# A fused attention and two expert layers: the first expert's weights loaded at the moment the expert is chosen

## The chip, the core and the metric

The kernel runs on one core of a Trainium2 chip. The core has five engines that run in parallel, each in its own program order: PE (matmul), DVE (vector), ACT (scalar), POOL (GpSimd) and SP (here only an issuer of DMAs). DMAs are issued by SP, by ACT or by POOL and run beside the engines. The metric is device time in microseconds from start to end of one launch, the median of several; less is better.

## The reference

What must be computed, cut to what matters (B=8 batches, H=8 heads, S=576, D=64, 32 packed queries; N=4608 tokens of 512, E=8 experts, F=1024):

```python
p_packed = sm_attn(p, k, v)             # 32 packed queries attend to all keys, per batch and head
x = sm_attn(q, p_packed, p_packed)      # every query attends to the 32 packed results
x = x.transpose(0, 2, 1, 3).reshape(N, 512)

logits = x @ w_gate                     # layer 1: greedy routing over the flattened, sorted logits,
for idx in argsort(-logits.flatten()):  # each token to one expert, at most cap = N // E = 576 per expert
    tok, e = idx // E, idx % E
    if assigned[tok] < 0 and counts[e] < cap: assigned[tok] = e; counts[e] += 1
out[tokens of e] = relu(x @ w1[e]) @ w2[e]

logits = out @ w_gate2 + bias[modality] # layer 2: best expert per token, no capacity
out[tokens of e] = softmax_weight * (relu(x @ w1[e]) @ w2[e])
```

## The kernel before

**Attention.** Function `attention` loops over the eight batches. Each turn of its loop holds several batches at different stages: scores of the packed queries for batch i, the queries' scores for batch i-1, softmax and transposes for batch i-2. The last turn (i = 7) also holds `early()` (line 454), which is `nearest(0, 0, 20)` of the router (lines 670 to 678): seven DVE steps that find, for the first 20 of 36 token columns, the best expert, its code and the four bytes of its logit. It stands ahead of `pack_D` (line 242, tile `dup`) and of the transposition in `sm_aT` (line 338). After the loop the rows of attention's result are made: `out_rows` multiplies on PE (line 367), copies the result to the tile `xm` on ACT (line 370) and stores it to the DRAM tensor `xs` with a DMA on SP's queue (line 372): 40 stores, five for each batch.

**Routing.** `Router.phase(k)` finds the k-th expert to be filled: `nearest`, then `search`, eight rounds of one threshold comparison on DVE (`ge`), a count on PE (line 654), sums on DVE (`two`, `cp`), a second PE product (line 1008, `cp` with `oner`) and a reduction on DVE (`cmx`). After round eight the expert's number is written to `ex`. Then a list of its tokens (`idx`) is made. All these steps are recorded and have line 1008 where they are emitted later.

**Experts.** `forward` runs units: units 0 to 7 are the experts of layer 1 in the order in which they are chosen, later units are blocks of layer 2. For a unit POOL gathers its rows from `xs` into tile `G` (line 1263), PE transposes them (line 1300), ACT and DVE split them in a high and a low part, XH and XL (lines 1301 and 1302). The weights come as raw chunks of 512 KB into four buffers, `raw`; ACT copies a chunk to the high part (w1H, line 1460), and DVE (or POOL for w2) subtracts to get the low part (w1L, line 1466). The products of the first matrix are on line 1517, those of the second on line 1572; results of the first are evacuated by ACT and DVE (lines 1492 and 1494), those of the second by ACT (line 1577). For unit 0 the four chunks of the first matrix are loaded as 16 DMAs of 128 KB (line 1407), issued by SP after it has read the expert's number from `ex` into a register (line 1229).

**What sets the order.** The program is emitted once, by a list scheduler (`Sched`) that keeps a modelled time for each engine: whenever modelled PE time goes on (`advance`), it takes ready steps from its chains (routing, splits, gathers) and puts them between the products. Order on each engine is fixed then; on the chip an engine that comes to a step whose data isn't there waits, with all behind it. `due` is the modelled time at which a chunk has landed, `GLAND` (8.5) the modelled time between the first gather and unit 0's first transposes.

**Memory and semaphores.** `raw` lies in the pool `m_w`, which is opened after attention's pools are closed, so it lies on memory that attention's tiles held; its first DMA waits for all that used them, the row stores of line 372 among it. The completions of DMAs issued by SP and ACT are counted on eight semaphores, DMAHW0 to DMAHW7, that are given out in turn in program order over both queues; a DMA first waits until the one that had its semaphore before it has landed.

Of the kernel before, what the change touches and what calls it, by code (L numbers as in the profile page):

```python
# [7 lines left out]
F32 = mybir.dt.float32  # L8
# [9 lines left out]
B, H, S, D, NP = 8, 8, 576, 64, 32  # L18
N, DM, E, F = 4608, 512, 8, 1024
# [40 lines left out]
def attention(tc, ctx, cn, q, k, v, p, w_gate, xs, LG, middle, early):  # L60
    nc = tc.nc
# [273 lines left out]
    def sm_aT(b):  # L335
        T, mx, T3 = Ts.pop(b)
        a = new_aT(b)
        nc.vector.transpose(out=a, in_=T)
        aT[b] = a
# [21 lines left out]
    def out_rows(b, c, ring, hook=None):  # L361
        ahead(b, c)
        n = 128 if c < 4 else 64
        dst = wk.tile([128, 4, 4, 32], F32, name="xm", bufs=5)[:n]
        t = ring.tile([128, 4, 4, 32], F32, name="tr")[:n]
# [5 lines left out]
        to = xs[b * S:b * S + 512].rearrange("(p m) d -> m p d", m=4)[c] if c < 4 else xs[b * S + 512:(b + 1) * S]  # L371
        nc.sync.dma_start(to, dst.rearrange("p a c i -> p (a c i)"))
        if c == 4:
# [9 lines left out]
    todo = [(b, c) for b in range(B) for c in range(5)]  # L383
# [18 lines left out]
    for i in range(B):  # L402
# [43 lines left out]
        if p1 and SM == 1:  # L446
            sm_max(i - 1)
            sm_sub(i - 1, nc.gpsimd)
        if EARLY and not n1 and EP == 1:
            early()  # L450
        pack_v(i)
        fill(FILL[2])
        pack_D(i)
        if p2 and AT == 0:
            sm_aT(i - 2)
        if AP == 2:
            ahead(*todo[0])
# [673 lines left out]
BYROW = 5  # L1131
EARLY = 20
EP = 1
# [15 lines left out]

def forward(tc, ctx, cn, R, R2, wg2, S, P, todo, rows, closing, xs, ys, lst, out, m1_w1, m1_w2, m2_w1, m2_w2):  # L1150
    nc = tc.nc
# [9 lines left out]
    def more_phases():  # L1161
        k = phase_k[0]
        if k < E and k <= min(started[0] + 3, P.coded + 2):
            phase_k[0] += 1
            P.add(k)

    for b, c in todo:
        half = 0.44 + (SLACK1 if P.coded >= 0 else SLACK) / 2
        rows(b, c, lambda: S.advance(half))
        S.advance(half)  # L1170
# [4 lines left out]
    W = {n: wp.tile([128, 4096], F32R, name="w" + n) for n in ("1H", "1L", "2H", "2L")}  # L1175
    raw = wp.tile([128, 4, 1024], F32, name="raw")
    raws = [raw[:, i] for i in range(4)]
    mp = ctx.enter_context(tc.tile_pool(name="m_ps", bufs=1, space=PSUM))
# [17 lines left out]
    gathered, l1_done, lg_done = [0], [-1], [-1]  # L1196
    free = list(raws)
    queue = []
    landed, due = {}, {}

    class Unit:
# [16 lines left out]
        def prepare(self):  # L1218
# [8 lines left out]
            else:  # L1227
                t, i = R2.tb[:, 0], self.u - E
            self.e = nc.values_load(t[0:1, i:i + 1], engines=[SP], min_val=0, max_val=E - 1)
            if not self.one:  # L1230
# [17 lines left out]
                if self.last:  # L1248
                    cm.ops.append(("vector", 0.1, lambda: nc.vector.tensor_copy(sa, Ma[:, :, 1]), t))
            for which in (1, 2):  # L1250
                queue.extend((self, which, c) for c in range(4))
# [146 lines left out]
    def fetch():  # L1398
        while queue and free:
            u, which, c = queue[0]  # L1400
            w = ((m1_w1, m1_w2) if u.one else (m2_w1, m2_w2))[which - 1]
            if which == 1 and (not u.u or 2 <= u.u < BYROW):
                queue.pop(0)
                t = free.pop(0)
                rows = w[bass.ds(u.e, 1)].rearrange("o (c a i) f -> a c i (o f)", a=4, i=32)[c]
                for i in range(4):
                    nc.sync.dma_start(t[32 * i:32 * i + 32], rows[i])
                landed[u.u, which, c] = t
                due[u.u, which, c] = S.t["sync"] = max(S.t["sync"], S.t["tensor"] + (2 if u.u else LAND)) + 2.2
                continue  # L1410
# [279 lines left out]
def tile_attention_moe(ctx, tc, q, k, v, p, m1_wg, m1_w1, m1_w2, mod_id, m2_wg, m2_bias, m2_w1, m2_w2, out):  # L1690
# [7 lines left out]
    LG = rp.tile([128, NT, E], F32, name="LG")  # L1698
    HL = rp.tile([128, 2, NT], BF16, name="HL")
    wg2 = rp.tile([128, 4, 32], F32, name="wg2")  # L1700
    ctx.enter_context(tc.manual_schedule())
# [19 lines left out]
    P.add(0)  # L1721
    forward(tc, ctx, cn, R, R2, wg2, S, P, todo, rows, attn.close, xs, ys, lst, out, m1_w1, m1_w2, m2_w1, m2_w2)

# [21 lines left out]
```

## Time and profile before

| | us |
|---|---|
| time, median of 3 runs (lowest, highest) | 1134.14 (1133.48, 1136.73) |
| the profiled execution's own time | 1134.52 |
| its span, first to last instruction | 1132.8 |
| PE busy | 1041.8 (92%) |
| DVE busy | 713.5 (63%) |
| POOL busy | 488.7 (43%) |
| ACT busy | 444.6 (39%) |

The profile is of one execution. Attention fills the first 189 us of the span, layer 1 goes from 213 to about 702, layer 2 from there to the end. A share over the whole span says little about a stage; the views below are therefore of stretches. The chain of waits is followed back from the last instruction, at each step to what released it; read forward it tells which work set the end.

### The profile page before, as it was taken

The numbers are of one execution on the slowest core, as the hardware profiler recorded it, in microseconds if no ns is written. First come the engines' busy times: TensorE is split into PE (matmuls) and PEld (weight loads), VectorE is DVE, ScalarE is ACT, GpSimd is POOL, SyncE is SP. The second block draws the span as 40 slices with busy tenths as digits, with TensorE's granted clock in tenths as the row PEclk, the third lists the DMA queues.
The fourth block names the chain that finished last, engine by engine and source line by source line (L and its number), as shares of the span: only waits on it lengthen the run. The fifth ranks groups of instructions, "written<-read, shape, count | busy, mean of one in ns | idle before, by whom it ended". The sixth has DMA issues, their size and how long they took to land.

```text
span 1132.8 us, 24490 instructions
## 1 busy us (share of the span) xinstructions
PE 1041.8 (92%) x9152; PEld 967.9 (85%) x9152; DVE 713.5 (63%) x2105; ACT 444.6 (39%) x940; POOL 488.7 (43%) x595
## 2 busy tenths in 40 slices
PE   6689797699899998999999999989999999999996
PEld 4577664588888897989999999979898999999995
DVE  1468777688979889884556566655555556455430
ACT  4467564323332323333434334333443433434331
POOL 1123301212424224047565344477787778742401
PEclk9899899699999999999999999999999999999998
DMA  9989246633243242224345343554445454433301
GB/s 257 278 228 259 53 168 201 158 75 117 64 139 113 80 137 57 99 89 145 117 134 138 99 145 93 135 143 126 126 144 143 106 170 136 127 125 102 99 20 43
DMA packets 117857, 146.90 MB, mean 130 GB/s; under 512 B 55946, under 2 KB 80522, under 8 KB 116704
## 3 DMA queue, kind: packets, MB, share of 16 engines
q1 hardware_dynamic: 102368, 116.43, 35.9%
q0 software_dynamic: 13776, 28.76, 8.7%
q8 instruction: 74, 1.21, 0.5%
q14 instruction: 55, 0.45, 0.2%
q10 hardware_dynamic: 1584, 0.05, 0.1%
HBM read 116.31 MB, written 29.52 MB: 129 GB/s over the span
## 4 chain that ended last, share of the span: by engine, by line
PE 60%; DVE 12%; issue 9%; DMA 9%; POOL 5%; ACT 2%; SPq 2%; POOLq 0%; ACTq 0%; DVEq 0%
PE mm L1572 26%; PE mm L1517 22%; DMA G<-ys,gi 4%; POOL out_dram L1344 3%; PE sc L170 2%; POOL G L1282 2%; PE tr L367 1%; DMA raw<-in_moe_w_dram 1%; PE sc L367 1%; DVE hL L1494 1%; DMA G<-xs,idx 1%; DMA vm<-in_v_dram 1%; PE tr L150 1%; DVE cmx L1008 1%; PE b L150 1%
## 5 line engine op out<-in xcount | busy, mean ns | idle before, releaser
L1517 PE MATMUL mm<-XH,w1H 128*128 128x290 f32 (+3 forms) x1024 | 306.9, 300 | 8.7 <-ACT XH L1301 3.8
L1517 PE MATMUL mm<-XL,w1H 128*128 128x290 f32 (+3 forms) x1024 | 307.9, 301 | 0.5 <-DVE XL L1321 0.3
L1517 PE MATMUL mm<-XH,w1L 128*128 128x290 f32 (+3 forms) x1024 | 305.4, 298 | 2.8 <-DVE w1L L1466 2.7
L1572 PE MATMUL mm<-hH,w2H 128*128 128x288 f32 (+3 forms) x768 | 231.9, 302 | 1.1 <-ACT YT L1577 1.1
L1572 PE MATMUL mm<-hH,w2L 128*128 128x288 f32 (+3 forms) x768 | 232.7, 303 | 0.0
L1572 PE MATMUL mm<-hL,w2H 128*128 128x288 f32 (+3 forms) x768 | 231.7, 302 | 0.1
L1492 ACT ACTIVATE hH<-mm 128x290 fp32r<-128x290 f32 (+3 forms) x256 | 105.7, 413 | 293.4 <-PE mm L1517 279.6
L1517 PEld LDWEIGHTS mm<-XH,w1H 128*128 128x128 f32 x1024 | 195.2, 191 | 11.2 <-ACT XH L1301 4.2
L1517 PEld LDWEIGHTS mm<-XH,w1L 128*128 128x128 f32 x1024 | 195.4, 191 | 3.9 <-DVE w1L L1466 3.5
L1517 PEld LDWEIGHTS mm<-XL,w1H 128*128 128x128 f32 x1024 | 194.7, 190 | 1.6 <-DVE XL L1321 0.8
L1494 DVE SCALAR_TENSOR_TENSOR hL<-mm,hH 128x290 fp32r<-128x290 f32 (+3 forms) x256 | 115.2, 454 | 116.7 <-ACT hH L1492 115.6
L1282 POOL DMA_INDIRECT G<-ys,gi x152 | 158.2, 1041 | 62.8 <-issue 31.7
L1572 PEld LDWEIGHTS mm<-hH,w2H 128*128 128x128 f32 x768 | 144.5, 188 | 1.6 <-ACT YT L1577 1.5
L1572 PEld LDWEIGHTS mm<-hL,w2H 128*128 128x128 f32 x768 | 144.5, 188 | 0.3 <-DVE hL L1494 0.3
L1572 PEld LDWEIGHTS mm<-hH,w2L 128*128 128x128 f32 x768 | 144.4, 188 | 0.1
L1344 POOL DMA_INDIRECT out_dram<-Y,si x93 | 96.1, 1033 | 112.0 <-DVE Y L1542 48.5
L1466 POOL TENSOR_TENSOR w2L<-raw,w2H 128x512 fp32r<-128x512 f32 x48 | 63.2, 1338 | 172.2 <-ACT w2H L1460 172.1
L1577 ACT ACTIVATE YT<-mm 128x288 f32<-128x288 f32 (+2 forms) x96 | 39.9, 419 | 203.8 <-PE mm L1572 202.1
L1308 DVE STREAM_TRANSPOSE XT<-G 128x128 f32<-128x128 f32 x206 | 55.6, 295 | 83.6 <-DMA G<-ys,gi 62.0
L1466 DVE TENSOR_TENSOR w1L<-raw,w1H 128x512 fp32r<-128x512 f32 x128 | 83.8, 677 | 19.6 <-ACT w1H L1460 19.0
L1460 ACT ACTIVATE w1H<-raw 128x512 fp32r<-128x512 f32 x128 | 73.1, 623 | 19.5 <-DMA raw<-in_moe_w_dram 11.5
L1460 ACT ACTIVATE w2H<-raw 128x512 fp32r<-128x512 f32 x128 | 73.1, 622 | 0.0
(383 smaller groups left out, 1544.3 us busy)
## 6 DMA issues: line engine op xcount, KB each, us to landing
raw<-in_moe_w_dram SPq DMA_DIRECT2D x112, 512.0 KB
ys<-Y SPq DMA_DIRECT2D x8, 1152.0 KB
qm<-in_q_dram SPq DMA_DIRECT2D x8, 1024.0 KB
vm<-in_v_dram SPq DMA_DIRECT2D x8, 1024.0 KB
xs<-xm SPq DMA_DIRECT2D x32, 256.0 KB
raw<-in_moe_w_dram SPq DMA_DIRECT2D x64, 128.0 KB
km<-in_k_dram SPq DMA_DIRECT2D x7, 1024.0 KB
G<-ys,gi POOLq DMA_INDIRECT x152
```

The source lines that it names most:

```text
L150: nc.tensor.transpose(t[:, i, :], src[:, h + i // 2, 128 * (i % 2):128 * (i % 2) + 128], ident)
L170: nc.tensor.matmul(t[32 * c:32 * c + 32, :512].rearrange("p (i j n) -> p j i n", i=2, j=2)[:, j], lhs(h, j), m[:, h], start=True, stop=Tru ...
L1282: nc.gpsimd.indirect_dma_start(out=G[:, g], out_offset=None, in_=ys[:n], in_offset=bass.IndirectOffsetOnAxis(ap=self.gi[:, g:g + 1], axis= ...
L1308: nc.vector.transpose(out=self.x[0][:, :, 32 * g:32 * g + 32], in_=G[:, g].rearrange("p (c i) -> p c i", c=4))
L1344: i = nc.gpsimd.indirect_dma_start(out=to, in_=rows, in_offset=None, out_offset=bass.IndirectOffsetOnAxis(ap=at, axis=0), bounds_check=to. ...
L1460: nc.scalar.activation(a, b, AF.Copy)
L1466: (nc.gpsimd if pool else nc.vector).tensor_tensor(p[0], p[1], p[2], op=OP.subtract)
L1492: nc.scalar.activation(hh, t, AF.Relu)
L1494: ch.ops.append(("vector", 0.37, lambda: nc.vector.scalar_tensor_tensor(hl, t, 0.0, hh.bitcast(F32), op0=OP.max, op1=OP.subtract), ts + 0.2))
L1517: nc.tensor.matmul(t, a[:, c, fs], b[:, c, s], start=(i == 0), stop=(i == 11))
L1572: nc.tensor.matmul(t, l, r, start=(i == 0), stop=(i == 23))
L1577: nc.scalar.activation(YT[:, d, s], t, AF.Copy)
```

## The change

It has three parts. The raw buffers get memory of their own (pool `r_s`, opened at the start). `first_loads` issues the expert's number and the 16 loads of unit 0 when phase 0 has chosen its expert (`P.hooks` are called by `choose`), and the row stores of the last batch go to ACT's queue. `early()` stands after `pack_D` and `sm_aT`.

```diff
-        nc.sync.dma_start(to, dst.rearrange("p a c i -> p (a c i)"))
+        (nc.scalar if b == B - 1 else nc.sync).dma_start(to, dst.rearrange("p a c i -> p (a c i)"))
...
-        if EARLY and not n1 and EP == 1:
-            early()
         pack_v(i)
         fill(FILL[2])
         pack_D(i)
         if p2 and AT == 0:
             sm_aT(i - 2)
+        if EARLY and not n1 and EP == 1:
+            early()
...
+    raws = [raw[:, i] for i in range(4)]
+    queue, landed, due, one_e = [], {}, {}, []
+
+    def load_rows(u, e, c, t):
+        w = m1_w1 if u < E else m2_w1
+        rows = w[bass.ds(e, 1)].rearrange("o (c a i) f -> a c i (o f)", a=4, i=32)[c]
+        for i in range(4):
+            nc.sync.dma_start(t[32 * i:32 * i + 32], rows[i])
+        landed[u, 1, c] = t
+        due[u, 1, c] = S.t["sync"] = max(S.t["sync"], S.t["tensor"] + (2 if u else LAND)) + 2.2
+
+    def first_loads():
+        if one_e or 0 not in P.experts:
+            return
+        one_e.append(nc.values_load(R.ex[0:1, 0:1], engines=[SP], min_val=0, max_val=E - 1))
+        for c in range(4):
+            load_rows(0, one_e[0], c, raws[c])
+
+    P.hooks.append(first_loads)
...
-    raw = wp.tile([128, 4, 1024], F32, name="raw")
-    raws = [raw[:, i] for i in range(4)]
...
-    free = list(raws)
-    queue = []
-    landed, due = {}, {}
+    free = []
...
-            for which in (1, 2):
+            for which in (1, 2) if self.u else (2,):
                 queue.extend((self, which, c) for c in range(4))
...
+    raw = rp.tile([128, 4, 1024], F32, name="raw")
```

On SP, at the end of attention, the last two row stores stand ahead of the expert's number and the first load. Before:

```order
L372 DMA xs_70<-xm_2427 128x512 [waits DMAHW6_49,Activation_49]
L372 DMA xs_70<-xm_2435 64x512 [waits DMAHW7_49,Activation_49]
L1229 TENSOR_LOAD ex_378 [waits DVE_49]
L1229 ISA x2
L1407 ISA
L1407 DMA raw_2458<-in_moe_w1_dram 32x1024 [waits DMAHW3_49,DMAHW2_49,DMAHW4_49,DMAHW1_49,DMAHW5_49,DMAHW0_49,DMAHW6_49,DVE_49,DMAHW7_49,PE_49,Pool_49]
```

The same place on SP in the changed kernel; the two stores are the last of batch 6, and the loads are those of line 1407 before (ISA rows put the register into a DMA's address):

```order
L372 DMA xs_70<-xm_2383 128x512 [waits DMAHW1_49,Activation_49]
L372 DMA xs_70<-xm_2392 64x512 [waits DMAHW2_49,Activation_49]
L1181 TENSOR_LOAD ex_379 [waits DVE_49]
L1181 ISA x2
L1174 ISA
L1174 DMA raw_78<-in_moe_w1_dram 32x1024 [waits DMAHW4_49]
L1174 ISA
L1174 DMA raw_78<-in_moe_w1_dram 32x1024 [waits DMAHW6_49]
```

The five stores of the last batch are gone from SP's order and the first load waits for one semaphore. On ACT they stand each behind its copy of line 370, ahead of the first w1H. In the order of both queues the stores and the loads take the semaphores in turn: of the 16 loads (counted from 0), load 3 waits for the last store of batch 6, loads 5, 7, 9 and 11 for the second to the fifth store of batch 7, the others for earlier loads.

On DVE, in the last turn of attention's loop (`best`, `rw`, `mxc`, `sign`, `key`, `digits` are the nearest-expert step), before:

```order
L319 TENSOR_REDUCE mx<-T 128x36
L670 TENSOR_REDUCE best_1874<-LG 128x20
L671 TENSOR_TENSOR rw<-LG,best_1874 128x160
L672 TENSOR_TENSOR rw<-rw,w8b 128x160
L673 TENSOR_REDUCE mxc_1875<-rw 128x20
L675 TENSOR_SCALAR sign<-best_1874 128x20
L677 TENSOR_TENSOR key<-best_1874,sign 128x20
L678 CAST digits_1876<-key 128x4x20
L242 TENSOR_SCALAR dup<-b_66,st 128x128 x2
L338 STREAM_TRANSPOSE qm<-T 128x1152
```

The same place in the changed kernel:

```order
L319 TENSOR_REDUCE mx<-T 128x36
L242 TENSOR_SCALAR dup<-b_66,st 128x128 x2
L338 STREAM_TRANSPOSE qm<-T 128x1152
L670 TENSOR_REDUCE best_1920<-LG 128x20
L671 TENSOR_TENSOR rw<-LG,best_1920 128x160
L672 TENSOR_TENSOR rw<-rw,w8b 128x160
L673 TENSOR_REDUCE mxc_1921<-rw 128x20
L675 TENSOR_SCALAR sign<-best_1920 128x20
L677 TENSOR_TENSOR key<-best_1920,sign 128x20
L678 CAST digits_1922<-key 128x4x20
```

The seven steps stand behind `dup` and the transposition instead of ahead of them.

On DVE, where unit 0 begins (w1L is the low part of its weights, XL of its rows, hL of its first results; the other rows are rounds of the search for the second expert), before:

```order
L1008 TENSOR_SCALAR w<-w,sel_f 128x36
L1008 TENSOR_TENSOR ge<-w,tab 128x15x5x8
L1466 TENSOR_TENSOR w1L<-raw,w1H 128x512
L1008 TENSOR_TENSOR two<-b_66,own 128x64
L1466 TENSOR_TENSOR w1L<-raw,w1H 128x512 x4
L1302 TENSOR_TENSOR XL<-mm_2462,XH 128x4x128
L1302 TENSOR_TENSOR XL<-mm_2463,XH 128x4x128
L1008 TENSOR_REDUCE two_2113<-two 128x8
L1494 SCALAR_TENSOR_TENSOR hL<-mm_2464,hH 128x256
```

The same place in the changed kernel (lines 1477, 1318 and 1505 are 1466, 1302 and 1494 before):

```order
L1008 TENSOR_TENSOR cp<-two_2114,fold_361 128x120
L1477 TENSOR_TENSOR w1L<-raw,w1H 128x512
L1008 TENSOR_REDUCE cmx<-b_66 128x15
L1008 SCALAR_TENSOR_TENSOR cmx,sel_f<-cmx,onef 128x15
L1477 TENSOR_TENSOR w1L<-raw,w1H 128x512 x4
L1318 TENSOR_TENSOR XL<-mm_2488,XH 128x4x128
L1318 TENSOR_TENSOR XL<-mm_2489,XH 128x4x128
L1008 TENSOR_SCALAR wt<-w,sel_f 128x36
L1505 SCALAR_TENSOR_TENSOR hL<-mm_2490,hH 128x256
```

Before, three rounds and the first part of a fourth stand ahead of unit 0's first XL; in the changed kernel it is one round and most of a second. From the second half of unit 4 on, both orders are the same on every engine.

## Rows read from the trace of the kernel before

**Rows 1.** Chain of waits, end of attention to unit 0: start us, us, what.
```profile
189.34 3.44 DMA xs<-xm
...
192.92 0.38 SPq L1407
...
196.98 6.26 DMA raw<-in_moe_w_dram
203.26 6.70 DMA raw<-in_moe_w_dram
...
210.72 1.29 DVE w1L L1466 x2
212.02 1.21 DVE XL L1302 x2
...
213.27 2.93 PE mm L1517 x12
```

**Rows 2.** Stretches: length, busy us by engine, PEclk, DMA share, GB/s.
```profile
184.30:188.60 4.30, 4.30 (x21) 3.02 (x20) 3.54 (x16) 2.59 (x5) 0.00 (x0) 1.00 0.62 218
188.60:192.90 4.30, 1.08 (x39) 0.97 (x38) 4.01 (x18) 0.59 (x1) 0.00 (x0) 1.00 0.47 154
...
197.30:203.30 6.00, 1.82 (x12) 1.15 (x12) 4.15 (x14) 1.15 (x2) 2.31 (x3) 0.50 0.98 217
203.30:207.70 4.40, 1.66 (x11) 1.53 (x12) 2.54 (x8) 1.15 (x2) 0.00 (x0) 0.50 1.03 241
```

**Rows 3.** Timeline of DVE, the last attention turn: start us, us, instruction [idle before].
```profile
132.31 0.30 DVE L670 TENSOR_REDUCE best<-LG 128x20 f32<-128x160 f32 x1
...
135.85 0.60 DVE L242 TENSOR_SCALAR dup<-b,st 128x128 f32<-128x128 f32 x2
136.37 1.37 DVE L338 STREAM_TRANSPOSE qm<-T 128x1152 f32<-128x1152 f32 x1
```

**Rows 4.** Timelines of ACT and PE, the same turn.
```profile
134.62 1.16 ACT L326 ACTIVATE T<-T 128x1152 f32<-128x1152 f32 x1 [0.62 <-POOL T L323]
137.04 0.78 ACT L256 ACTIVATE qz<-tr 64x256 f32<-64x256 f32 x2 [1.25 <-PE tr L250]
...
138.93 0.62 PE L170 MATMUL sc<-qT,qz 128*32 128x256 f32 x2
```

**Rows 5.** Timelines of DVE and POOL, an earlier attention turn.
```profile
90.95 0.60 DVE L242 TENSOR_SCALAR dup<-tr,st 128x128 f32<-128x128 f32 x2
...
91.11 2.13 POOL L323 TENSOR_TENSOR T<-T,mx 128x1152 f32<-128x1152 f32 x1 [2.34 <-DVE mx L319]
```

**Rows 6.** Timelines of DVE and SP, an expert's number and the loads behind it.
```profile
183.35 0.15 DVE L1008 TENSOR_SCALAR ex<-code 128x1 int32<-128x1 f32 x1
...
241.93 0.14 DVE L1008 TENSOR_SCALAR ex<-code 128x1 int32<-128x1 f32 x1
...
243.03 1.90 SPq L1417 DMA_DIRECT2D raw<-in_moe_w_dram  x4
```

**Rows 7.** Timeline of ACT: a DMA issue, last row copy, unit 1's weights.
```profile
131.21 0.41 ACTq L1008 DMA_DIRECT2D wg<-in_moe_w_gate_dram  x1
...
188.72 0.59 ACT L370 ACTIVATE xm<-sc 64x512 f32<-64x512 f32 x1 [0.41 <-PE sc L367]
...
257.99 1.14 ACT L1460 ACTIVATE w1H<-raw 128x512 fp32r<-128x512 f32 x2
```

**Rows 8.** Timeline of POOL: the first gather; of DVE: two rounds' comparisons.
```profile
193.69 1.36 POOL L1263 DMA_INDIRECT G<-xs,idx  x1 [49.09 <-DVE oh L1008]
...
193.56 0.46 DVE L1008 TENSOR_TENSOR ge<-w,tab 128x600 bf16<-128x600 bf16 x1
196.77 0.47 DVE L1008 TENSOR_TENSOR ge<-w,tab 128x600 bf16<-128x600 bf16 x1
```

**Rows 9.** Stretches: unit 0's and unit 3's first halves, columns as in rows 2.
```profile
213.00:248.00 35.00, 32.27 (x243) 31.18 (x243) 26.04 (x84) 11.28 (x26) 10.23 (x8) 0.94 0.17 41
...
417.00:452.00 35.00, 29.40 (x282) 27.87 (x273) 33.35 (x124) 9.78 (x23) 16.10 (x18) 1.00 0.27 78
```

More of the change, by code (lines that the diff above doesn't have):

```diff
@@ L1147, with forward @@
 LCAP = N + -(-IG // 2) * 64
-def forward(tc, ctx, cn, R, R2, wg2, S, P, todo, rows, closing, xs, ys, lst, out, m1_w1, m1_w2, m2_w1, m2_w2):
+def forward(tc, ctx, cn, R, R2, wg2, S, P, raw, todo, rows, closing, xs, ys, lst, out, m1_w1, m1_w2, m2_w1, m2_w2):
     nc = tc.nc
@@ L1228, in prepare @@
                 t, i = R2.tb[:, 0], self.u - E
-            self.e = nc.values_load(t[0:1, i:i + 1], engines=[SP], min_val=0, max_val=E - 1)
+            self.e = (nc.values_load(t[0:1, i:i + 1], engines=[SP], min_val=0, max_val=E - 1) if self.u
+                      else one_e[0])
             if not self.one:
@@ L1401, in fetch @@
             w = ((m1_w1, m1_w2) if u.one else (m2_w1, m2_w2))[which - 1]
-            if which == 1 and (not u.u or 2 <= u.u < BYROW):
+            if which == 1 and 2 <= u.u < BYROW:
                 queue.pop(0)
[L1404 to L1409, printed above, removed]
+                load_rows(u.u, u.e, c, free.pop(0))
                 continue
@@ L1721, in tile_attention_moe @@
     P.add(0)
-    forward(tc, ctx, cn, R, R2, wg2, S, P, todo, rows, attn.close, xs, ys, lst, out, m1_w1, m1_w2, m2_w1, m2_w2)
+    forward(tc, ctx, cn, R, R2, wg2, S, P, raw, todo, rows, attn.close, xs, ys, lst, out, m1_w1, m1_w2, m2_w1, m2_w2)
 _INS = ["q", "k", "v", "p", "moe_w_gate", "moe_w1", "moe_w2", "moe2_modality_id", "moe2_w_gate", "moe2_modality_bias",
```

## The prediction

> **What bounds the kernel now.** I read the chain of waits first, around the end of attention, and then the table of stretches and the timelines of single engines for the price of each link. The chain runs through a gap [rows 1]: the last row store is issued at 189.34 and lands 3.44 us later, SP issues the first weight load at 192.92, two spans of weight loads follow (6.26 and 6.70 us, to 209.96), then the last w1L and XL, and PE begins unit 0 in earnest at 213.27. From 197.3 to 207.7 PE is busy for 3.5 of 10.4 us, at a granted clock of 0.50, the 1.2 GHz level, while the DMA engines are busy all the time at 217 to 241 GB/s [rows 2]. So a load of 2.1 MB holds everything. It could start earlier: the expert's number is written at 183.50 [rows 6], 9.4 us before the first load, which only waits because its buffer lies on attention's memory. While attention ends, the DMA engines are 0.62 busy [rows 2]; there is room.
>
> **The moved step.** All times here and below are on the clock of the trace before. The nearest-expert step occupies DVE from 132.31 until `dup` starts at 135.85, 3.54 us [rows 3]. Then come the transposes of `dup`, ACT's two `qz` copies at 137.04 and PE's next scores at 138.93 [rows 4]. Without the step ahead of it `dup` can start at about 132.4, since the products it reads are done. It isn't slowed by POOL's subtraction of that time: in an earlier turn the same pair took 0.60 us beside it [rows 5]. The gain isn't 3.54, as ACT does its exponentials first, until 134.62 + 1.16 = 135.78 [rows 4]. So `qz` runs from 135.8 to 136.6 instead of to 137.8, and the scores, which had also waited for the transposition ending at 137.74 [rows 3] and the products behind it, start at about 136.9 instead of 138.93: 2.0 us. The step itself now runs behind the transposition, from 134.3 to at most 134.3 + 3.5 = 137.8. If it takes so long, the logits' transposes behind it on DVE (about 1.2 us) and the reduction after them start 0.7 us later than they otherwise would, so I bound the gain by 1.3 and 3.5 us and take **-2.0**. PE's rows, ACT's copies and phase 0 all hang on these scores and move with them.
>
> **The loads.** SP now reaches the expert's number behind batch 6's last store, whose copy is ACT's sixth from the end; that store goes out at about 184.6 (an estimate: ACT's copies follow each other by some 0.8 us back from 188.72 [rows 7]), and with 0.3 us for it and the 0.96 us that SP needed from number to load at unit 1 (242.07 to 243.03 [rows 6]), the first load goes out at about 186.0. Sixteen at 0.48 us (four in 1.90 [rows 6]) would be out by 193.7, but loads 5, 7, 9 and 11 wait for stores of the last batch. These now cost ACT five issues of about 0.41 us [rows 7], and ACT had gaps of some 0.4 us between its copies there [rows 7], so the last copy slips from 188.72 by about 0.5, the last store goes out at about 189.9 and, at 3.44 us [rows 1], lands at 193.3, half a microsecond later than before. Load 11 can go then, and the last by 195.7. The gather waits for the same store: 194.2 instead of 193.69 [rows 8].
>
> How much lands when? Stores alone ran at 218 GB/s with the DMA engines 0.62 busy [rows 2], which is 352 GB/s if full. The last batch's 1.18 MB (four stores of 256 KB and one of 128) thus take 3.4 us of the engines, and of the 7.3 us from 186.0 to 193.3 there are 3.9 left for loads: 0.92 MB at 235 GB/s (between the two saturated stretches of rows 2). Of 2.10 MB 1.18 remain. Until the gather's data flow, about 195.3, another 0.47 MB come; the other 0.71 MB share the engines with the gather's 1.18 MB, at half of 235, and take 6.0 us: 201.3 instead of 209.96, **-8.7**. From there to unit 0 it was 3.3 us [rows 1], and it stays so: 204.6 instead of 213.27.
>
> Bounds. At its best the loads are no limit and DVE's own order is one. The first w1H waits for the last store too (193.3) and takes some 0.6 us; then DVE has one round of 3.2 us [rows 8], most of a second (2.6), eight w1L of 0.65 and two XL of 1.21 together [rows 1]. The last four w1L stand together behind the rounds. If the first four vanish in the rounds' waits for PE this is 193.9 + 3.2 + 2.6 + 2.6 + 1.2 = 203.5, if none does 206.1. So -9.8 at the best, and 204.6 lies between. At its worst all that is asked for is served in turn at the lower rate: 3.4 us for the stores, then 2.10 + 1.18 MB and 0.52 MB of the first w2 chunk at 217 GB/s, 17.5 us, so the loads are there at 206.9: -3.1.
>
> The rows give 3.44 us for a store with no loads beside it. The Trainium skill (DMA: Bandwidth & Descriptors, section "Issuing engines are not separate DMA queues") says that DMAs started by different engines run on the same 16 DMA engines and interleave, so ACT's queue would bring the stores no bandwidth of their own. By that rule the last store, 128 KB at half of 235 GB/s instead of the whole, lands 0.5 us later, gather and load 11 go 0.5 us later, and the loads' term is -8.2 instead of -8.7; no row of before has stores and loads in flight together, so the trace can't say.
>
> What hides behind this cover: the raw buffers' 16 KB come out of memory that attention didn't need, and the loads ask for nothing of PE or DVE; both cost nothing. The second matrix's first chunk is asked for once w1L has freed a buffer, as before.
>
> **What it gives back.** The gap wasn't empty. Before, three and a half rounds of the search for the second expert ran in it; now it is one and most of a second, and two more rounds stand in unit 0's first half. The lag is one round from there to unit 4. A round is 3.21 us on DVE from comparison to comparison [rows 8]; it is busy 26.04 of 35 us in unit 0's first half, but 33.35 in unit 3's [rows 9], where nothing fits in any more. So between 0 and 6.4 us (two rounds in full) come back; since DVE has 9.0 us free where both rounds land, I take a bit over a third, **+2.3**.
>
> **Sum.** -2.0 - 8.7 + 2.3 = -8.4 us. The profiled execution took 1134.52 (span 1132.8 and 1.7 around it), so 1126.1; the median of the runs lies 0.4 lower, so I predict **1125.7**. After unit 4's first half both orders are equal, and layer 2 should only shift.
>
> **Rivals.**
>
> The DMA engines are the bound whichever queue asks first. For: they are at 0.98 to 1.03 from 197.3 on [rows 2]. Against: from 188.6 to 192.9 they were 0.47 busy and brought no weights [rows 2]; that hole is filled now. It would give -2.0 - 3.1 + 2.3 = -2.8: 1131.3.
>
> The routing eats it: the displaced rounds come back in full, because units 1 to 3 have first halves bound by DVE (29.40 of 35 us busy on PE, 33.35 on DVE [rows 9]). -2.0 - 8.7 + 6.4 = -4.3: 1129.8. Against: it is a round once, not a round per unit.
>
> The change doesn't do what it says: the loads still end up behind the last stores, over SP's order or over the shared semaphores. Then only the moved step counts: 1132.1. Against: of 16 loads five can be held by the last store at all.
>
> Slower: unit 1's weights come late. The search's end moves by four of the eight last result blocks of unit 0's first half, some 7 us relative to the products; on ACT six w1H of unit 1 stand ahead of evacuations of unit 0's second half. Unit 1's first w1H ran 257.99 - 242.07 = 15.9 us after its number was known [rows 6, 7]; in the new order I count 15. SP's 0.96 us and 2.1 MB at 235 GB/s need 9.9, so there are 5 to spare. The case decides from where these loads take over 14 us: then ACT stands, result banks fill and PE stands in that and each later unit up to the fourth. At 3.1 us in each of four units 12.4 us are lost against 8.4 won: 1138.1.
>
> **How the numbers follow.** Forecast 0.68 (its own range 1121.5 to 1129.0), DMA engines 0.12, routing 0.12, not done 0.04, slower 0.04. The best that the bounds make is -3.5 - 9.8 + 0 = -13.3, 1120.8; all at their best at once is unlikely, and I stop at 1121.0. Upward the DMA case must be in. Range 1121.0 to 1131.5, which leaves out the last two cases and about 0.1 of the others. About 0.3%, 3.4 us, can be told from no change, so faster means below 1130.7: the forecast (0.68), the routing case nearly whole (0.11) and half of the DMA case (0.06), 0.85; slower the last case, 0.04; the same 0.11.
>
> **What would show it.** The moved step: `dup` straight behind the reduction of line 319, scores of the last batch about 2 us earlier. The loads: first load at about 184 on the new trace, the last landed at about 199, unit 0's products steady from about 202.5. The return: PE's idle time in units 0 to 3 up by about 2 us, and unit 5 beginning about 8.4 us earlier. I'm wrong if the loads are spread out to 204 or later, if the last store lands much later than 3.4 us after its issue, or if units 0 to 3 together grow by more than 4 us.

## The result, and the profile after

| us | before | changed |
|---|---|---|
| median of 20 runs each (one of before, of 2549.71, is not in the ratio) | 1136.84 | 1124.23 |
| the profiled execution's own time | 1134.52 | 1123.10 |
| its span | 1132.8 | 1121.4 |

The ratio is 0.989 with a 95% interval of 0.9872 to 0.9908, so 12.5 us faster (10.5 to 14.6) out of 1136.84. The first three runs of before, on which the prediction was built, lay 2.7 lower. The time 1125.7 was predicted, 8.4 below the base; the spans differ by 11.4. So the time was met, but the gain of 8.4 lies below the interval of the measured one, and three of its terms were not met.

Eight of the experiments (e1 to e5, e8 to e10) ran while the kernel before took 1356 to 1357 us, at a mean granted clock of 0.89 instead of 0.97 and with pauses of PE that the profile gives no cause for (145 us ahead of the experts' products in e1), most of it in layer 1's later units and layer 2; their times stand beside those of the kernel before run with them, and across such runs only distances up to unit 0 are compared.

**The moved step.** Timelines of DVE and PE in the last attention turn of the changed kernel (start us, us, instruction; `mx` of line 319 is what stands ahead of the step):

```profile
130.48 1.28 DVE L319 TENSOR_REDUCE mx<-T 128x36 f32<-128x1152 f32 x1
131.80 0.61 DVE L242 TENSOR_SCALAR dup<-b,st 128x128 f32<-128x128 f32 x2
...
133.62 0.28 DVE L670 TENSOR_REDUCE best<-LG 128x20 f32<-128x160 f32 x1
133.93 0.33 DVE L671 TENSOR_TENSOR rw<-LG,best 128x160 bf16<-128x160 f32 x1
...
136.00 0.38 PE L170 MATMUL sc<-qT,qz 128*32 128x256 f32 x1
...
138.10 2.00 PE L367 MATMUL tr<-bd,aT 128*128 128x256 f32 x8
```

And before, beside [rows 3] and [rows 4]:

```profile
131.10 1.29 DVE L319 TENSOR_REDUCE mx<-T 128x36 f32<-128x1152 f32 x1
...
142.62 2.00 PE L367 MATMUL tr<-bd,aT 128*128 128x256 f32 x8
```

`dup` takes 0.61 us beside POOL's subtraction, as in [rows 5], and the scores start 5.52 us behind the reduction. Before, the reduction stood at 131.10 and the scores at 138.93 [rows 4], 7.83 behind it. That is the forecast gain, 2.3 instead of 2.0. But the first row product (`tr`) came 3.69 us behind the first scores before and comes 2.10 behind them now. The stretches of the scores, before and changed (us, busy us of PE, PEld, DVE, ACT and POOL, granted clock, DMA share, GB/s):

```profile
138.93:142.60 3.67, 3.67 (x68) 3.15 (x61) 3.25 (x9) 0.00 (x0) 0.13 (x1) 0.57 0.00 0
```

```profile
136.00:138.10 2.10, 2.10 (x62) 1.62 (x62) 1.97 (x5) 0.00 (x0) 0.00 (x0) 1.00 0.00 0
```

PE was busy all through both: before, mostly at the 1.2 GHz level, now at 2.4. So attention's rows begin 3.9 us earlier against the reduction, not 2.0.

The step itself became shorter too. Before, its product of line 671 stood beside POOL's subtraction (timelines of DVE and POOL):

```profile
132.64 2.13 DVE L671 TENSOR_TENSOR rw<-LG,best 128x160 bf16<-128x160 f32 x1
132.46 2.13 POOL L323 TENSOR_TENSOR T<-T,mx 128x1152 f32<-128x1152 f32 x1 [1.97 <-DVE mx L319]
```

It took 2.13 us there and ended 0.18 behind the subtraction; in the changed kernel it starts as that one ends (133.98) and takes 0.33. So it is in all profiles: 2.13 in the three with the step in its old place, 0.32 to 0.33 in the eleven with it moved. The whole step took 3.5 us before and takes 1.8 now, to 135.42.

**The loads.** Chain of waits of the changed kernel, end of attention to unit 0 (it answers to [rows 1]):

```profile
183.26 5.08 DMA xs<-xm
...
191.27 2.19 DMA raw<-in_moe_w_dram
193.46 1.50 POOL G L1279
...
195.27 5.46 DMA G<-xs,idx
...
200.78 1.13 PE mm L1316 x4
...
201.93 0.61 ACT XH L1317
...
202.58 3.44 PE mm L1528 x13
```

The chain before ran through the weights and their low parts; now it runs through the gather and the gathered rows. Timelines of ACT and SP there (the last SP row is one of the 16 loads, number 11 of the front's count, which waits for the last row store):

```profile
184.78 0.61 ACT L370 ACTIVATE xm<-sc 64x512 f32<-64x512 f32 x1 [0.46 <-ACT xm L370]
185.42 0.52 ACTq L372 DMA_DIRECT2D xs<-xm  x1
192.57 3.31 ACT L1471 ACTIVATE w1H<-raw 128x512 fp32r<-128x512 f32 x6 [7.19 <-DMA raw<-in_moe_w_dram]
197.02 1.15 ACT L1471 ACTIVATE w1H<-raw 128x512 fp32r<-128x512 f32 x2 [1.13 <-DMA raw<-in_moe_w_dram]
...
182.12 12.42 SPq L1174 DMA_DIRECT2D raw<-in_moe_w_dram  x16
...
192.20 0.32 SPq L1174 DMA_DIRECT2D raw<-in_moe_w_dram  x1
```

The first load goes out at 182.12, the last chunk is there by 197.02. But the last row store, issued at 185.42 behind six of the sixteen loads, lands only shortly before 192.20, 6.8 us later; before it took 3.44 [rows 1]. The gather waits for it and starts at 193.44, 8.66 us behind the last row copy instead of 4.97. The chain names a load as what released the gather; but POOL's wait for the store's semaphore ends at 192.21, with those of SP and ACT, and in all fourteen profiles the gather starts 0.9 to 1.3 us behind that store's landing. The first w1H waits for it too, since its tile lies on attention's memory. Stretches of the changed kernel, columns as above:

```profile
184.80:189.10 4.30, 1.02 (x38) 0.85 (x37) 4.01 (x20) 0.59 (x1) 0.00 (x0) 0.93 0.96 273
189.10:193.40 4.30, 0.45 (x5) 0.29 (x5) 0.57 (x3) 0.83 (x2) 0.00 (x0) 0.50 0.58 182
```

The DMA engines, 0.62 busy while attention ended [rows 2], are full there now, and what is lost is behind it, from 189.1 to 193.4: SP waits for the stores with the other loads, DVE is busy 0.57 of 4.30 us. Unit 0's steady products begin at 202.58 instead of 213.27.

**What came back.** Units 0 to 3 (to the first logits product of line 1361, 1377 now) in the kernel before, with PE's waits over all four:

```profile
213.27:280.26 66.99, 63.66 (x525) 60.39 (x525) 51.37 (x171) 21.30 (x47) 14.95 (x13) 0.97 0.33 87
280.26:348.17 67.91, 61.86 (x550) 58.57 (x549) 58.22 (x220) 21.27 (x47) 21.13 (x23) 1.00 0.29 93
348.17:416.38 68.21, 63.99 (x599) 60.93 (x596) 59.07 (x212) 20.43 (x47) 25.98 (x28) 0.97 0.38 112
416.38:484.14 67.76, 61.60 (x558) 58.96 (x556) 60.54 (x210) 20.69 (x47) 16.24 (x18) 1.00 0.29 91
```

```profile
PE b L1008 <- DVE AB L1008: 4.2, 3, 1.9
PE mm L1300 <- DMA G<-xs,idx: 2.0, 4, 1.2
PE b L1008 <- DVE cp L1008: 1.9, 5, 0.7
```

The same in the changed kernel (waits: us in total, times, longest):

```profile
202.58:269.90 67.32, 65.30 (x528) 61.46 (x528) 50.46 (x170) 22.32 (x49) 15.36 (x13) 0.95 0.33 87
269.90:339.78 69.88, 61.76 (x553) 58.44 (x552) 59.85 (x217) 20.90 (x47) 21.00 (x23) 1.00 0.37 103
339.78:408.51 68.73, 64.18 (x597) 60.87 (x596) 57.93 (x220) 20.50 (x47) 25.41 (x28) 0.98 0.34 100
408.51:472.71 64.20, 61.52 (x561) 58.66 (x559) 58.14 (x213) 20.61 (x47) 16.43 (x19) 1.00 0.35 106
```

```profile
PE b L1008 <- DVE cp L1008: 3.5, 6, 1.7
PE mm L1316 <- DMA G<-xs,idx: 3.1, 3, 1.6
```

Units 0 to 2 are 2.8 us longer, unit 3 is 3.6 us shorter: together -0.7. The waits of the rounds (`cp`) and of the rows grew; those for `AB`, a step of making an expert's list, are gone altogether. In unit 3 alone PE's listed waits fall from 6.4 to 2.8 us, those for `AB` from 1.9 to none.

### The profile page after: what moved, and what is told of

Same layout as the page of the kernel before. It is cut to its first block, busy times and chain, and to the rows that moved or that the text cites. A ratio compares the mean times of both kernels' runs of the same rounds, so it can differ in the third digit from the quotient of the medians.

```text
span 1121.4 us, 24489 instructions
## 1 busy us (share of the span) xinstructions
PE 1041.9 (93%) x9152; PEld 968.1 (86%) x9152; DVE 707.4 (63%) x2105; ACT 444.8 (40%) x940; POOL 487.9 (44%) x595
## 4 chain that ended last, share of the span: by engine, by line
PE 58%; DVE 12%; DMA 9%; issue 9%; POOL 7%; ACT 2%; SPq 2%; POOLq 0%; ACTq 0%; DVEq 0%
PE mm L1583 24%; PE mm L1528 22%; DMA G<-ys,gi 4%; POOL G L1298 3%; POOL out_dram L1360 3%; PE sc L170 2%; PE tr L367 1%; DMA G<-xs,idx 1%; DVE hL L1505 1%; PE tr L150 1%; PE sc L367 1%; DMA vm<-in_v_dram 1%; POOL lst L973 1%; PE mm L1316 1%; PE b L150 1%
## 5 line engine op out<-in xcount | busy, mean ns | idle before, releaser
L1477 DVE TENSOR_TENSOR w1L<-raw,w1H 128x512 fp32r<-128x512 f32 x128 | 83.6, 677 | 19.6 <-ACT w1H L1471 19.1
L1279 POOL DMA_INDIRECT G<-xs,idx x25 | 25.2, 1009 | 110.6 <-DMA raw<-in_moe_w_dram 53.3
## 6 DMA issues: line engine op xcount, KB each, us to landing
raw<-in_moe_w_dram SPq DMA_DIRECT2D x64, 128.0 KB
```

Source lines behind the costliest of these rows:

```text
L1279: nc.gpsimd.indirect_dma_start(out=r.rearrange("p a d -> p (a d)"), out_offset=None, in_=xs, in_offset=bass.IndirectOffsetOnAxis(ap=phases ...
L1477: (nc.gpsimd if pool else nc.vector).tensor_tensor(p[0], p[1], p[2], op=OP.subtract)
```

## The experiments

All distances are from the timelines, in us: from the start of the reduction of line 319 to the first scores; from there to the first row product; from the start of the last row copy `xm` (of line 370) to the start of the gather and to unit 0's first product; the last column is gather to product.

| kernel | scores | to row product | gather | unit 0 | gather to unit 0 |
|---|---|---|---|---|---|
| before | 7.83 | 3.70 | 4.97 | 23.51 | 18.5 |
| changed | 5.52 | 2.10 | 8.66 | 17.80 | 9.1 |
| changed, again (e14) | 5.52 | 2.10 | 8.25 | 17.69 | 9.4 |
| step alone (e1) | 5.52 | 2.10 | 5.01 | 22.84 | 17.8 |
| step alone, again (e15) | 5.52 | 2.10 | 4.93 | 23.44 | 18.5 |
| changed without the step (e2) | 7.83 | 3.20 | 8.83 | 18.50 | 9.7 |
| stores on SP (e3) | 5.52 | 2.10 | 14.12 | 23.30 | 9.2 |
| loads held until the store lands (e4) | 5.52 | 2.10 | 4.56 | 23.70 | 19.1 |
| loads held until it is issued (e5) | 5.52 | 3.78 | 4.47 | 21.31 | 16.8 |
| one chunk early (e6) | 5.52 | 2.10 | 7.25 | 16.71 | 9.5 |
| memory alone (e8) | 7.83 | 4.14 | 5.10 | 21.66 | 16.6 |
| four big loads (e9) | 5.52 | 2.10 | 9.90 | 18.77 | 8.9 |
| four, two of them held (e10) | 5.52 | 2.10 | 8.28 | 17.27 | 9.0 |
| no loads at the end (e13) | 5.52 | 2.10 | 4.37 | 13.69 | 9.3 |

Two theories were on trial. About the loads: that **bytes in flight ahead of it delay the last row store, and the gather behind it has become what unit 0 waits for**, against that ACT's queue or SP's waits are to blame. About the step: that it is worth 3.9 us, against 2.0.

### The step alone (e1, e15)

```diff
# of the kernel before
-        if EARLY and not n1 and EP == 1:
-            early()
         pack_v(i)
...
             sm_aT(i - 2)
+        if EARLY and not n1 and EP == 1:
+            early()
```

> The kernel before with the nearest-expert step moved behind dup and the transposition, and nothing else. Theory A (the step is worth what the two traces show): the last turn's scores come 2.3 us earlier and run at the 2.4 GHz level, so that the first row product comes 3.9 us earlier than in the kernel before (about 138.7 on its clock, against 142.62), last xm at about 184.8, and, the order of everything else being the same, the time falls by 3.9 us. Theory B (the term of the prediction): the scores come 2.0 us earlier, still at the 1.2 GHz level, and the rows follow: 2.0 us.

> The kernel before with the step alone moved, once more, for its time on a chip that isn't held at a lower clock in layer 1. First scores 5.5 us and, at the 2.4 GHz level, first row product 7.6 us behind the reduction of line 319; last row copy 53.7 us behind it instead of 57.6; unit 3 as long as in the kernel before (67.8 us). Theory A (two thirds of the time won are the loads', one third the step's): 3.5 to 4 us faster than the kernel before, ratio 0.9965. Theory B (the prediction's term): 2.0 us, ratio 0.998.

Both give 5.52 and 2.10, so 3.9 us to the row products, and the last row copy 53.7 us behind the reduction instead of 57.6. The times can't tell: 1354.53 against 1357.27 (ratio 0.997, 0.9947 to 0.9993) and 1133.00 against 1135.01 (0.9977, 0.9957 to 0.9997), so 4.1 us (1.0 to 7.2) in e1 and 2.6 us (0.3 to 4.9) in e15, and both theories lie in both intervals. In e15's profile the units took part of it back; its units 1 and 3, of the same order as before:

```profile
274.60:344.52 69.92, 63.17 (x550) 60.10 (x549) 58.31 (x220) 21.25 (x47) 21.07 (x23) 0.98 0.28 90
...
412.45:481.47 69.02, 63.04 (x558) 60.41 (x556) 60.49 (x210) 20.70 (x47) 16.19 (x18) 0.98 0.30 90
```

They are 2.0 and 1.3 us longer than in the kernel before and had a clock of 0.98 where that one had 1.00; unit 1 also waited 1.0 us more for the gathered rows.

### Everything but the step (e2)

```diff
# of the changed kernel
+        if EARLY and not n1 and EP == 1:
+            early()
         pack_v(i)
...
             sm_aT(i - 2)
-        if EARLY and not n1 and EP == 1:
-            early()
```

> The changed kernel with the nearest-expert step back in its old place. Theory A: the loads, their memory and the order are worth 6.8 us up to unit 0 and 11.4 - 3.9 = 7.5 us at the end; 3.9 us slower than the changed kernel. Theory B: they are worth 8.7 us up to unit 0, and the time is 2.0 us above the changed kernel.

Scores at 7.83 again, as before, and gather and unit 0 within 0.8 us of the changed kernel: the parts hardly touch each other. Time 1346.88 against 1357.27 (0.9919, 0.9886 to 0.9951), so 11 us less with an interval of 6.7 to 15.5, too wide to tell 7.5 from 9.4. The stretches tell more: with the step in its old place the scores took 3.20 us, not 3.70, and in e5, with the step moved, 3.78. Their stretches, e2 and e5:

```profile
137.75:140.90 3.15, 3.15 (x69) 2.81 (x62) 2.73 (x8) 0.00 (x0) 0.00 (x0) 0.66 0.00 0
```

```profile
138.03:141.80 3.77, 3.77 (x62) 2.58 (x62) 2.99 (x7) 0.00 (x0) 1.10 (x1) 0.55 0.00 0
```

So 2.3 us of the step are always there, and up to 2 more hang on the clock's level in just these 3 us. In the kernel before PE had stood idle for 3.0 us where the clock fell; in e5 it had not (its longest wait there is 1.0), and the clock fell all the same. In the three profiles with the step in its old place it was low in the scores each time, in the eleven with it moved once. What makes it fall there stays open.

### The loads held until the last store has landed (e4), or is issued (e5)

```diff
# of the changed kernel: load_rows
-        for i in range(4):
-            nc.sync.dma_start(t[32 * i:32 * i + 32], rows[i])
+        def issue():
+            for i in range(4):
+                nc.sync.dma_start(t[32 * i:32 * i + 32], rows[i])
+        if u or c < HELD:
+            issue()
+        else:
+            held.append(issue)
# forward, behind the last row store (the first line in e4 alone)
+    nc.scalar.activation(cn["lastxm"][0], cn["onef"][:64, :1], AF.Copy)
+    nc.scalar.activation(raw[:, HELD:, :1], cn["onef"][:, :4 - HELD].unsqueeze(2), AF.Copy)
+    for issue in held:
+        issue()
```

HELD is 0 in both. ACT's small write to `raw` stands behind the last store's issue, and in e4 behind a write to the stored tile, which waits for its landing.

> The changed kernel, with all 16 loads of unit 0 held until the last row store has landed; nothing else is moved. Theory A (the loads in flight make the last store late): without them it lands some 3.5 us after its issue (185.4), so the gather starts at about 190.0 instead of 193.44; the loads go from about 189.2 and need 17 us as in the kernel before, unit 0's products start at about 209.5 instead of 202.6, and the time is some 7 us above the changed kernel's. Theory B (a store on ACT's queue takes 6.8 us whatever else runs): gather at 193.4, loads from 192.4 to 209.4, unit 0 at 212.8, some 10 us above the changed kernel's. Beside it: the order of DVE's and PE's steps is the changed one, so the time against that of the kernel before with the step alone moved tells what the new order of the search rounds gives or costs: +2.8 us by units 0 to 2, -3.5 us by unit 3.

> The changed kernel, with the 16 loads held only until the last row store has been issued on ACT's queue (from about 186.3). Theory A: the store's data stand ahead of the loads' and it lands 3.5 to 4.5 us after issue; the gather starts at 190 to 191 (2.5 to 3.4 us earlier than in the changed kernel), the loads land by about 200, unit 0 starts at 202.5 to 204.5: 0 to 2 us above the changed kernel. Theory B: the store still lands 6.8 us after its issue, the gather starts at 193.4, the loads land by about 200 to 203, unit 0 at 203.5 to 206.

Chain and POOL's timeline of e4:

```profile
183.12 2.82 DMA xs<-xm
...
189.93 6.95 DMA raw<-in_moe_w_dram
196.90 7.01 DMA raw<-in_moe_w_dram
```

```profile
187.04 1.26 POOL L1291 DMA_INDIRECT G<-xs,idx  x1 [48.49 <-DVE oh L1009]
```

With no load in flight the store on ACT's queue lands after 2.82 us; the rival theory falls. The gather starts 4.56 us behind the row copy, but now the loads are late and bound unit 0 as before. In e5 the store lands after 2.93 us although all sixteen loads are asked for right behind it, and the rest is the same in smaller: gather at 4.47, unit 0 at 21.31, later than the 17.7 to 19.7 us that its expectation amounts to (202.5 to 204.5, less 184.78), since the 16 loads took 17.7 us beside the gather (first issued at 189.88, last w1H at 207.57). Its time was 1345.59 against 1357.27 (0.9934, 0.9903 to 0.9965).

Both have the changed kernel's order in units 0 to 3. Their unit 3 took 65.7 and 65.8 us; with the order of before it took 68.0 (e1) and 68.1 (e8) at that clock. At the higher one it was 64.2 in the changed kernel, in e14, e6 and e13, and 67.8 and 69.0 in before and e15. So unit 3's gain is the order's, whenever the loads come. e4 began unit 0 1.4 us later than e1, counted from the reduction, and was yet 6.0 us faster in the median (0.9939, 0.9912 to 0.9965, beside 0.997); the intervals just overlap.

### The stores back on SP's queue (e3), and the memory alone (e8)

```diff
# e3, of the changed kernel
-        (nc.scalar if b == B - 1 else nc.sync).dma_start(to, dst.rearrange("p a c i -> p (a c i)"))
+        nc.sync.dma_start(to, dst.rearrange("p a c i -> p (a c i)"))
# e8, of the kernel before
-    raw = wp.tile([128, 4, 1024], F32, name="raw")
...
+    raw = rp.tile([128, 4, 1024], F32, name="raw")
```

> The changed kernel with the last batch's row stores on SP's queue again. There the last store stands behind all 16 loads. Theory A (SP's order is a bound of its own, as the part on ACT's queue supposes): the loads go out at 0.5 us each from about 185 and wait for each other's semaphores, so the last store goes out at 193 to 196 and lands at 197 to 200, the gather starts 5 to 7 us later than in the changed kernel (18.7 instead of 8.7 us at most behind the last row copy, 14 at least), unit 0 likewise, and the time is 5 to 8 us above the changed kernel's. Theory B (the DMA engines are the bound whichever queue asks): the same bytes go through, unit 0 starts within 2 us of the changed kernel's.

> The kernel before with the raw buffers in memory of their own and nothing else. The loads still stand behind the last store on SP, but need not wait for its landing: the first goes out some 1 us after that store's issue instead of 3.6. Theory A: they start 2.6 us earlier and all else follows, unit 0 and the end 2 to 2.6 us earlier than before; the store, whose data stand ahead of theirs, still lands 3 to 3.5 us after its issue. Theory B (with the gather beside them the loads take as much longer as they start earlier): unit 0 less than 1 us earlier.

Chain of e3:

```profile
192.55 2.91 DMA xs<-xm
195.57 0.64 ACT w1H L1471
...
196.37 1.58 POOL G L1279
```

The last store waits behind 16 loads in SP's order and goes out at 192.55, the gather starts 5.5 us later than in the changed kernel, and so does unit 0. Theory A holds in the trace. The store itself took only 2.91 us: the loads had been asked for since 183.36, and most of them had landed. In time nothing is to be seen of the lateness: 1343.31 against 1355.87 (0.9918, 0.9892 to 0.9943), as much as e2 at that clock. The changed kernel itself has no run at it, so what e3 loses by the end isn't known.

In e8 the first load goes out 2.6 us behind the row copy instead of 4.2, and unit 0 comes 1.85 us earlier (21.66 instead of 23.51): between the theories, nearer to A. Its time is that of before (0.9989, 0.9962 to 1.0017). Memory of its own brings little by itself; the early start needs the hook as well.

### How many bytes ahead of the store (e9, e10, e6, e13)

```diff
# e9, of the changed kernel; e10 the same with HELD = 2
-        for i in range(4):
-            nc.sync.dma_start(t[32 * i:32 * i + 32], rows[i])
+        if not u:
+            nc.sync.dma_start(t, w[bass.ds(e, 1), 128 * c:128 * c + 128].rearrange("o p f -> p (o f)"))
+        for i in range(4) if u else ():
+            nc.sync.dma_start(t[32 * i:32 * i + 32], rows[i])
# e6: HELD = 1 with the 16 loads of the changed kernel
# e13, of the changed kernel, in the middle of attention, instead of the hook's loads
+    for c in range(4):
+        rows_0 = m1_w1[0:1].rearrange("o (c a i) f -> a c i (o f)", a=4, i=32)[c]
+        for i in range(4):
+            nc.sync.dma_start(raws[c][32 * i:32 * i + 32], rows_0[i])
```

In e9 and e10 the big loads bring the rows of unit 0's matrix in another order, so unit 0's results are not the reference's, and as layer 2 routes by them, only layer 1 is compared. Big loads in the right order were not tried.

> The changed kernel with unit 0's first matrix in four loads of 512 KB instead of sixteen of 128 KB. No load then waits on SP for a store of the last batch, and all 2.1 MB are asked for by about 184, ahead of the last four stores. Theory A (bytes in flight delay the last store): the last store lands at 192 to 194, so 6.5 to 8.5 us after its issue; the hole at 189 to 193.4, where the DMA engines were 0.58 busy, is gone, the weights are there by then, but the first w1H and the gather still wait for that store; unit 0 starts within 1.5 us of the changed kernel's (17.8 us behind the last row copy). Theory B (SP's waits for semaphores make the store and the gather late): the store lands 3.5 us after issue, the gather starts 3 us earlier, unit 0 2 to 3 us earlier.

> The changed kernel with unit 0's first matrix in four loads of 512 KB, two at once and two held until the last row store has been issued. Theory A (the last store waits for the bytes ahead of it, and the gather for the store): 1.05 MB less stand ahead of that store, it lands 4 to 5 us after its issue instead of 6.8, the gather starts 2 to 3 us earlier (6 to 6.5 instead of 8.7 us behind the last row copy), the two held chunks (1.05 MB) go at full rate before the gather's rows flow, and unit 0 starts 15 to 16.5 us behind the last row copy instead of 17.8: 1.5 to 3 us faster than the changed kernel. Theory B (loads beside the gather run at 190 GB/s, as where all were held until the store's issue): unit 0 at 18 to 20 us behind the last row copy, the same time or up to 2 us slower.

> The changed kernel, with the first four loads (one chunk) at once and the other twelve held until the last row store has been issued. Theory A (bytes ahead of the store): less stands ahead of it, it lands 3 to 4.5 us after its issue, the gather starts 5 to 6.5 us behind the last row copy, but twelve loads now run beside the gather at the 190 GB/s seen where all were held: their last lands some 14 us after they start, unit 0 at 18 to 20 us behind the last row copy against 17.8, so no gain. Theory B (an earlier gather is what unit 0 waits for): unit 0 at 15 to 16.5 us.

> The changed kernel, but unit 0's 16 loads fetch expert 0's first matrix instead of the chosen one, in the middle of attention, so that none is in flight when attention ends; unit 0's results are therefore not the reference's, and since layer 2 routes by them only times up to layer 1's end count. Theory A (the loads cost by making the last store, and with it gather and first w1H, late): the store lands 2.8 to 3.5 us after its issue, the gather starts 4.5 us behind the last row copy instead of 8.7, and unit 0 is then bound by DVE's order, some 10 us behind the first w1H: 14 to 14.8 us behind the last row copy instead of 17.8, so that the loads still cost 3 to 4 us. Theory B (DVE's rounds and w1L bound unit 0 already): 17 us or more, as DVE's rounds wait for nothing of it.

Chain of e9:

```profile
183.01 8.01 DMA xs<-xm
...
192.28 1.36 POOL G L1281
```

Chain of e13, and a stretch of it:

```profile
190.02 2.83 DMA xs<-xm
...
193.76 1.45 POOL G L1283
...
195.52 5.71 DMA G<-xs,idx
...
201.28 1.13 PE mm L1320 x4
```

```profile
193.00:197.00 4.00, 0.92 (x6) 0.58 (x6) 3.86 (x15) 4.00 (x8) 2.93 (x2) 0.52 0.15 47
```

The last store, with the megabytes of unit 0's loads that were asked for but hadn't moved when it was issued, and that moved until it landed (both counted from the traces' packets):

| kernel | open at its issue | moved until it landed | issue to landing, us |
|---|---|---|---|
| e4, e13 | 0 | 0 | 2.8 |
| e5 | 0 | 0.1 | 2.9 |
| e3 (on SP's queue) | 0.4 | 0.4 | 2.9 |
| e6 | 0.3 | 0.9 | 5.4 |
| changed, e14, e2 | 0.5 | 1.0 | 6.8, 6.4, 6.9 |
| e10 | 0.7 | 1.6 | 6.5 |
| e9 | 1.7 | 1.7 | 8.0 |

It grows with the bytes, though not in proportion (on ACT's queue the batch's earlier stores, late as well, stand ahead of it too), and it does so in e9, where SP has nothing to wait for. That settles the first theory; but what counts are the loads that move beside the store, those asked for after it among them, and not all that was asked for ahead of it. Without the loads unit 0 begins 13.69 us behind the row copy, so they still cost it 4.1. (In e13 attention's rows took 3.3 us longer, with the loads among them, so its time says nothing.)

From the gather's start to unit 0 it is 8.9 to 9.7 us in all eight kernels where the weights are there in time, in e13 as in the others. So unit 0's own loads don't slow the gather: in e13 none is in flight, and the DMA engines are 0.15 busy in the first microseconds. But in all eight the loads of the second matrix go out 1.7 to 2.4 us behind the gather's start (in e13 at 196.19); what these cost it was not tried, and where its 9 us go wasn't taken apart.

e6's expectation missed: twelve loads beside the gather didn't run at 190 GB/s, its weights were there 12.6 us behind the row copy (199.14 - 186.58), and unit 0 began at 16.71, between the theories. e10 gained 0.5 us on the changed kernel's 17.80 and not 1.5 to 3: the two held chunks move together with the store, and it is late again.

### The changed kernel again (e14)

> The changed kernel itself, for a comparison on the same chip as the experiments. The moved step: the first scores 5.5 us behind the reduction of line 319 and, where the granted clock stays at the 2.4 GHz level, the first row product 7.6 us behind it; gather 8.7 and unit 0 17.8 us behind the last row copy; unit 3 some 2 to 3.5 us shorter than in the order of before. Time against the kernel before: 0.985 to 0.992.

It ran beside e6 and e13: 1124.53 against 1136.50 (0.9894, 0.9869 to 0.9918). e6 had 1122.34 (0.9874, 0.9845 to 0.9903). Its unit 0 is 1.0 us earlier behind the row copy and its median 2.2 us lower, but the intervals overlap: e6 is the better candidate, not a proven one.

## Why the prediction was right, and where it was not

| term | forecast (bounds) | measured in the profiles |
|---|---|---|
| ahead of the step, where nothing changes | 0 | -0.6 |
| moved step | -2.0 (-3.5 to -1.3) | -3.9 |
| loads, to unit 0 | -8.7 (-9.8 to -3.1) | -6.2 |
| given back, units 0 to 3 | +2.3 (0 to +6.4) | -0.7 |
| sum | -8.4 | -11.4 |

The measured terms: the reduction at 130.48 instead of 131.10; 7.62 instead of 11.52 from it to the row products; from these to the steady products 202.58 - 138.10 = 64.48 instead of 213.27 - 142.62 = 70.65; the four units 270.13 instead of 270.87.

**The step.** Its path was right to 0.3 us: `dup` unslowed, ACT's exponentials as the next to be late, scores 2.3 us earlier. The lower bound of 1.3 took the moved step at up to 3.5 us; it took 1.8, since its product no longer stands beside POOL's subtraction. What failed is the sentence that rows, copies and phase 0 "move with them": it took the scores' own 3.7 us as fixed, though their stretch had a granted clock of 0.57, which a row of before would have shown. The bounds held only waits and no clock. That part isn't safe: of eleven profiles with the step moved one had the low level in the scores.

**The loads.** The step that failed is "the last store goes out at about 189.9 and, at 3.44 us [rows 1], lands at 193.3". ACT's five issues cost 0.6 us as forecast (0.5): from the first row product to the last copy it is 46.7 us instead of 46.1. But the store took 6.8 us, the second of the conditions under which I said I'd be wrong. The weights came as forecast, 12.2 us behind the last row copy (197.02 - 184.78); the prediction had 12.1 (201.3, the copy at 189.2). The term came out at -6.2 because the gather bound instead, which no rival had as its end. The rule of the Trainium skill (DMA: Bandwidth & Descriptors, section "Issuing engines are not separate DMA queues") holds here: 2.82 us alone and 6.8 among the loads, on the same queue of ACT's. My price of 0.5 us from it was too small, since I counted the store's own 128 KB at half the rate and not the loads that moved beside it and beside the stores ahead of it. The same section says that issuing from several engines saves only the time on the sequencer, usually small beside the DMA itself. In e3 that order on SP's sequencer was worth 5.5 us, because the store stood behind sixteen loads.

**The return.** Units 0 to 2 gave back 2.8 in this pair of profiles, close to the forecast, but that isn't shown to be the order's: they took 203.1 us before and 205.9 in the changed kernel, yet 204.6 in e15 with the old order and 204.4 to 204.7 in e14, e6 and e13 with the new. Unit 3, for which I said that nothing fits in any more, gained 3.6, and that came in every profile of the new order. The step that failed is the count: I counted the rounds that move in and not the waits that the new order takes away. The order was there to be read, and the `AB` waits stand in the trace of before; the lower bound of 0 had no reason behind it.

**The rivals.** Of "the DMA engines are the bound", the mechanism was half right: they do serve the stores late; but its 206.9 for the weights is 17.7 us behind the row copy, 5.5 too late. "The routing eats it" and "not done" fell with unit 3 and with the first load at 182.12. Unit 1's first w1H ran 13.8 us after its number (250.76 against 236.94) with no wait shown ahead of it: the slower case wasn't near.

So a total short by 3.0 us, out of errors of -1.9, +2.5, -3.0 and -0.6 us, and the base of three runs 2.7 us below the later median, which hides the shortfall. Unit 0's steady products came at 202.58, as forecast (about 202.5), because the first, second and last of these errors cancel. The direction of the step and of the loads, and their paths up to the store, were the profile's; the sign of the return was wrong, and that the time fell within 1.5 us was luck in good part.

## What to carry to other kernels

When loads are pulled forward into a gap, look at who else uses the DMA engines there: a small store that others wait for shares them with every load that moves until it lands (here up to 1.7 MB, and 8.0 us instead of 2.8). Price it by those bytes, and follow whoever waits for the store (here the gather) as the next bound. And when a change reorders a saturated stage, read the waits that the new order removes as carefully as the work that it adds.

## What was not expected of the hardware

- The granted clock of the same short stretch differs between executions with one and the same order ahead of it: 1.00 in the changed kernel's scores, 0.55 in e5's; 2.10 and 3.78 us for the same 32 large products.
- The start of the last reduction of line 319 lies between 128.0 and 133.9 us in the fourteen profiles, though no instruction ahead of it was edited; a change of 2 us can't be read from absolute times of two profiles, only from distances.
- One DVE product (line 671) took 2.13 us beside POOL's subtraction and 0.33 behind it, while DVE's `dup` took 0.60 to 0.61 us with that subtraction beside it or not.
